# Six triangular solves given whole to one engine each, and a start without 320 zero products

## The chip, the cores and the metric

One core of one Trainium2 chip (trn2) runs the whole program in one launch. The metric is device time in microseconds of one execution; smaller is better. The core has five engines that run their own instruction queues in order: TensorE (PE; matrix products into PSUM; its weight loads are listed apart, as PEld), VectorE (DVE), ScalarE (ACT), GpSimd (POOL) and SyncE (SP), which here issues nearly all the DMAs.

## The reference

Three layers follow each other. The first is a delta-rule attention with B, H, S, D = 4, 8, 768, 48, a recurrence over 768 tokens with a 48 x 48 state per head:

```python
k_n = k / (norm(k) + 1e-06)
for t in range(S):
    y[:, :, t] = einsum('bhd,bhde->bhe', q[:, :, t], state)
    v_old = einsum('bhde,bhd->bhe', state, k_n[:, :, t])
    state = state + beta[t] * einsum('bhd,bhe->bhde', k_n[:, :, t], v[:, :, t] - v_old)
```

Its output, 3072 tokens of 384 numbers, goes through a mixture of 8 experts (each takes exactly 384 tokens, assigned greedily by sorted router logits; ReLU between two matrices) and then through a dense layer, `silu(h @ w_in) @ w_out` with 2048 hidden numbers. All inputs are float32.

## The kernel before, in words

**Attention by chunks.** The 768 tokens are cut into 24 chunks of C = 32. Within a chunk the recurrence becomes a triangular system of 32 equations per head. For each chunk `prep` loads q and k (L371 and, for the first four chunks, L364) and splits them into two fp16 halves (L373 on ScalarE, L374 on VectorE), and DMAs copy the halves to other partitions (L379); `gram` multiplies k with k and q with k on TensorE (L396) and evicts (L403, L405, L409, L410). Each operand of a product is a pair of fp16 halves, so every product is made of three.

**The solves.** Four chunks make a group, six groups in all; `tgroup(g)` inverts the 32 x 32 triangular matrices of a group, all 128 of them at once: a partition holds one matrix. It transposes the gram numbers into L (L421, VectorE), works out the norms (L425 to L436), scales L (L439, VectorE), and prepares X: multiplication (L448), triangular mask (L451, always GpSimd), diagonal (L454, always GpSimd). Then for j = 1 to 30 it multiplies row j of L with column j of X (L462, into a scratch) and adds this to X (L465): n columns by 31 - j rows, where n is at most j. Each step needs the one before it. At the end X is transposed back (L468, VectorE, two instructions) and split into fp16 halves (L475, L477) for the steps.

There is one X for all groups, so L448 of a group waits for L468 of the group before. L exists twice.

`SPLIT` says who solves: before, the first 4, 5, 6 or 10 columns of X go to VectorE and the others to GpSimd. Columns don't depend on each other, and each engine has its own scratch, so the two parts run side by side.

**The steps.** `stage(c)` loads k and v of chunk c (L485), splits k (L488, L489), scales v (L492, on VectorE or GpSimd, whichever the planner finds earlier), and copies eleven pieces into slots for TensorE with four DMAs (L497, about 1 MB). The slots exist twice, so the copies for chunk c + 2 wait until step c has been read. `step(c)` is the recurrence itself, for two halves of the heads: state times k (L527) and times q (L537), the inverted matrix (L548), the new state (L563), the chunk's output (L574); between these are fp16 splits on ScalarE and VectorE (L502 and L503) or on ScalarE and TensorE (L507 to L510). `gate(c)` makes the router's logits. Step c + 1 needs the state of step c.

**Start.** At the beginning `shapes` has TensorE make ten lots of 32 products of a zero tile, in five array shapes (L212); the planner charges 1.0 us for a lot. Their results are not used. `warm` gives 300 more zero products (L192, 128 x 256), each at the lowest priority, which the planner puts where TensorE would have nothing to do.

**Order.** The order of the instructions of every engine is fixed before the run, by a list scheduler (`Plan.order`): each operation is entered with its engine or engines, a cost, what it reads and writes, and a priority; the one that is ready first and has the longest tail behind it goes next. For a VectorE operation of n elements the cost is 0.07 + 0.00104 n, for GpSimd 0.075 + 0.002 n, and from one operation to the next that needs it on the same engine 0.127 and 0.102 us are added. SyncE's DMA issues are planned in the same way and stand in one queue. On the chip each engine takes its own queue in that order; an instruction whose operands are late holds up those behind it.

**Experts and dense layer.** They follow on the same engines. Between attention and the first expert there is a search for the tokens of that expert, on VectorE mostly; the weights are loaded and split (L801 to L810 for the dense layer), part of it in buffers that take the place of attention's L and X.

Of the kernel before, what the change touches and what calls it, by code (L numbers as in the profile page):

```python
# [20 lines left out]
C = 32  # L21
# [10 lines left out]
N6 = 3  # L32
FH = 0.0
KF = 2
SPLIT = (
    (("DVE", 0, 6), ("Pool", 6, C)),
    (("DVE", 0, 5), ("Pool", 5, C)),
    (("DVE", 0, 4), ("Pool", 4, C)),
    (("DVE", 0, 5), ("Pool", 5, C)),
    (("DVE", 0, 4), ("Pool", 4, C)),  # L40
    (("DVE", 0, 10), ("Pool", 10, C)),
)
GROUPS = tuple(tuple(range(c, c + 4)) for c in range(0, NCH, 4))
SX, SWG = 6, 10

# [143 lines left out]
def warm(P, nc, bank, z, n, r, w):  # L189

    for _ in range(n):
        P.op("PE", WC, lambda e: nc.tensor.matmul(bank[:, 0:256], z[:, 0:128], z[:, 128:], start=True, stop=True),  # L192
             r=r, w=w, prio=-1e6, look=(1.0, 0.0))


def shapes(P, nc, banks, z, r, w):

    T = nc.tensor
    forms = (
        (1, lambda i: (slice(0, 128), slice(0, 128), 0)),  # L200
        (2, lambda i: (slice(64 * i, 64 * i + 64), slice(64 * i, 64 * i + 64), 0)),
        (2, lambda i: (slice(64 * i, 64 * i + 64), slice(0, 128), i)),
        (4, lambda i: (slice(32 * i, 32 * i + 32), slice(32 * i, 32 * i + 32), 0)),
        (2, lambda i: (slice(0, 128), slice(64 * i, 64 * i + 64), 0)),
    )

    for n, (k, form) in enumerate(2 * forms):
        def go(e, n=n, k=k, form=form):
            for j in range(32):
                rows, cols, b = form(j % k)  # L210
                at = 48 * (j // k % 8)
                T.matmul(banks[b][cols, at:at + 48], z[rows, 0:cols.stop - cols.start], z[rows, 128:176], start=True, stop=True)  # L212
        P.op("PE", 1.0, go, r=r, w=w, prio=HOT)


class Arena:


# [43 lines left out]
def act(n, sb=True):  # L262
    return 0.055 + 0.00083 * n + (0.043 if sb else 0.0)
# [10 lines left out]
def attention(tc, P, ar, sh, kq, kv, bt, cst, idh, wg, xs):  # L274
    nc = tc.nc
    V, A, G, T = nc.vector, nc.scalar, nc.gpsimd, nc.tensor
    E = {"DVE": V, "Pool": G}
# [29 lines left out]
    wz = ar.new(["wz"], [384], F16)  # L307
# [14 lines left out]
    def sta(t, at, Q):  # L322
        return t[:, at, Q // 4].rearrange("p s (i q) -> p (s i) q", q=4)[:, :, Q % 4]
# [12 lines left out]

    P.op("DVE", 0.2, lambda e: V.memset(wz, 0.0), w=["wz"])
    P.op("Pool", 0.1, lambda e: G.memset(tiny, 1e-30), w=["tiny"])
    shapes(P, nc, ar.banks[4:6], wz, ["wz"], [("y", 0), ("y", 1)])
    warm(P, nc, ar.banks[5], wz, WARM, ["wz"], [("y", 1)])  # L340
    P.op("DVE", 4.3, fill(gsl, "p x c g s n -> p (x c g s n)"), w=["gsl"])
    for t, k in ((rsl[1][:, 0:8], 1), (rsl[1][:, 8:], 1), (rsl[0][:, 0:8], 0), (rsl[0][:, 8:], 0)):
# [40 lines left out]
    def gram(c):  # L383
# [8 lines left out]
        def mm(e, Q):  # L392
            n = 0
            for t in range(2):
                for a, b in P3:
                    T.matmul(gp_[:, Q], sta(gs[:, x], 2 * a + t, Q), cv[:, :, b, t, Q // 4, :, Q % 4], start=(n == 0), stop=(n == 5))  # L396
                    n += 1
# [15 lines left out]
    def tgroup(g):  # L413
# [24 lines left out]
        for k in range(2):  # L438
# [3 lines left out]
             r=["nb0"], w=["nb1"])  # L442
        parts = [(k, en, k0, k1) for k, (en, k0, k1) in enumerate(SPLIT[g])]
        xk = [("X", k) for k in range(2)]
# [61 lines left out]
    def split_pe(hi, lo, acc, ident, s, n, kp, kh, kl):  # L506
        P.op("ACT", act(n, False), lambda e: A.activation(hi, acc, AF.Copy, scale=s), r=[kp], w=[kh])  # L507
        P.op("PE", 0.01 + n / 2400, lambda e: T.matmul(acc, ident, hi, start=False, stop=True, skip_group_check=True),
             r=["idl", kh], w=[kp])
        P.op("ACT", act(n, False), lambda e: A.activation(lo, acc, AF.Copy, scale=s), r=[kp], w=[kl])  # L510

    def step(c):
        x = c % 2
        rs, y = rsl[x], yp[x]
        for g in range(2):
            w_, u_, n_, wu_, st_ = wt[g], ut[g], ns[g], wu[g], st[g]

            def vin(e, g=g, wu_=wu_):
                T.matmul(wu_[:, 0], ids, kr[x][:, 8 + 4 * g:12 + 4 * g, :], start=True, stop=(c == 0))

            P.op("PE", 0.38, vin, r=["ids", ("kv", x, 0)], w=[("wu", g)], prio=LEAD["vin"])
            if c:
                def kn(e, bs, last, g=g, wu_=wu_, n_=n_):
                    for a, b in bs:
                        for Q in range(4):
                            for t in range(2):
                                T.matmul(wu_[:, 0, Q], sta(rs, KR[x] + 2 * a + t, 4 * g + Q), n_[:, b, t, Q, :],  # L527
                                         start=False, stop=(last and (a, b) == P3[-1] and Q == 3 and t == 1))
# [178 lines left out]
HOT = 1000.0  # L707
# [511 lines left out]
def _program(ins):  # L1219
    import concourse.bacc as bacc  # L1220

    nc = bacc.Bacc("TRN2", target_bir_lowering=False, num_devices=1)
    d = {k: nc.dram_tensor(f"in_{k}", a.shape, mybir.dt.from_np(a.dtype), kind="ExternalInput").ap()
         for k, a in ins.items()}
    out = nc.dram_tensor("out_0", _OUT, F32, kind="ExternalOutput").ap()
    with tile.TileContext(nc) as tc, ExitStack() as ctx:
        dram = ctx.enter_context(tc.tile_pool(name="dram", bufs=1, space=DRAM))
        xs = dram.tile([NTOK, 2 * DM], F16, name="xs")
        plan = Plan()
        ar = Arena(ctx, tc, plan, 212832)  # L1230
        ar.at(210852)
        sh = shared_tiles(ar)
        ar.at(0)
        plan.base, plan.look = 9.0 * HOT, LOOK
        attention(tc, plan, ar, sh, d["kq"], d["kv"], d["bt"], d["cst"], d["idl"], d["wg"], xs)
        moe(tc, plan, ar, sh, xs, d["w1"], d["w2"], d["win"], d["wout"], d["mch"], out)
        with tc.manual_schedule():
            plan.emit()
    return nc
# [22 lines left out]
```

## Time and profile before

| what | us |
|---|---|
| median of three runs (lowest, highest) | 1064.65 (1058.99, 1065.28) |
| the profiled execution | 1064.36 |
| its span, first to last instruction | 1062.7 |
| busy in the span: PE, PEld | 935.5, 676.6 |
| busy: DVE, ACT, POOL | 719.7, 491.1, 395.8 |
| PE busy with the 320 zero products | 7.9 |
| DVE busy with L462 and L465, 180 instructions each | 59.9, 62.1 |
| POOL busy with L462 and L465, 146 instructions each | 64.9, 71.5 |

Attention ends about 376 us into the span; the experts and the dense layer take the rest. Busy time is added up over the instructions of an engine. "Idle before" is idle time of the engine directly before an instruction, with what ended it; an instruction with little of it didn't hold its engine up. The granted clock of TensorE is a share of 2.4 GHz.

### The profile page before, as it was taken

To read this page: it belongs to the slowest core of one execution; us is meant where nothing else is said; L and a number is where in the kernel's file an instruction comes from. 1 tells how busy PE (TensorE), PEld (TensorE's weight loads), DVE (VectorE), ACT (ScalarE), POOL (GpSimd) and SP (SyncE) were. 2 spreads that over 40 slices of the span, in tenths; PEclk is the share of its full clock that TensorE was granted. 3 is DMA by queue.
4 is the path that set the end of the run, shared out by engine and by line. 5 is a ranking of instruction groups with operands and counts; after the bars stand their busy time and mean duration, and the time that the engine had idled before them with its cause. 6 is when DMAs were issued, how large, how long until landed. Compare 5 with 4: busy or idle time off the path is not lost.

```text
span 1062.7 us, 27011 instructions
## 1 busy us (share of the span) xinstructions
PE 935.5 (88%) x11073; PEld 676.6 (64%) x11073; DVE 719.7 (68%) x1852; ACT 491.1 (46%) x970; POOL 395.8 (37%) x515
## 2 busy tenths in 40 slices
PE   6987989988897831978998999998998999899997
PEld 6867889888887821544665565665665666566664
DVE  5898888888875587999558458558458457442250
ACT  4314446464555542656436337336336336742250
POOL 6578565747452253375204204203104103202011
PEclk9989899998988965898999999999999999999999
DMA  7428497877787736232203203103103104501000
GB/s 224 112 57 195 109 215 171 197 187 182 185 168 172 182 104 219 84 107 87 78 1 96 69 1 112 53 2 116 49 2 112 53 1 123 160 2 38 9 1 23
DMA packets 178796, 107.72 MB, mean 101 GB/s; under 512 B 141552, under 2 KB 162416, under 8 KB 178672
## 3 DMA queue, kind: packets, MB, share of 16 engines
q1 hardware_dynamic: 175600, 96.55, 35.3%
q0 software_dynamic: 3072, 9.44, 2.6%
q8 instruction: 87, 1.43, 0.5%
q14 instruction: 37, 0.30, 0.1%
HBM read 65.07 MB, written 9.44 MB: 70 GB/s over the span
## 4 chain that ended last, share of the span: by engine, by line
PE 56%; DVE 20%; DMA 9%; POOL 4%; issue 3%; SPq 3%; ACT 2%; POOLq 0%; DVEq 0%; ACTq 0%
PE bank L1138 44%; DMA sb<-sb 4%; PE bank L396 3%; SPq L497 2%; DVE sb L917 2%; DVE sb L465 2%; DVE sb L462 2%; PE bank L527 2%; DMA sb<-in_kv 2%; POOL sb L465 2%; POOL sb L462 1%; PE bank L537 1%; PE bank L563 1%; DMA sb<-in_kq 1%; DMA sb<-xs,sb 1%
## 5 line engine op out<-in xcount | busy, mean ns | idle before, releaser
L1138 PE MATMUL bank<-sb 128*128 128x384 f16 x3456 | 593.6, 330 | 0.0
L1138 PEld LDWEIGHTS <-sb 128*128 128x128 f16 x3456 | 328.4, 99 | 211.5 <-issue 11.8
L1178 POOL TENSOR_TENSOR sb<-sb 128x384 f16<-128x384 f32 x43 | 42.3, 984 | 301.3 <-ACT sb L1177 215.7
L1177 ACT ACTIVATE sb<-sb 128x384 f16<-128x384 f32 x128 | 66.3, 521 | 52.6 <-DVE sb L1175 51.5
L396 PE MATMUL bank<-sb 128*128 128x64 f16 x1152 | 75.4, 242 | 12.2 <-DVE sb L374 5.0
L396 PEld LDWEIGHTS <-sb 128*128 128x128 f16 x1152 | 72.4, 119 | 14.5 <-issue 14.2
L1175 DVE SCALAR_TENSOR_TENSOR sb<-bank,sb 128x384 f32<-128x384 f32 x128 | 69.7, 550 | 15.1 <-ACT sb L1174 14.7
L1174 ACT ACTIVATE sb<-bank 128x384 f32<-128x384 f32 x128 | 61.3, 480 | 33.0 <-PE bank L1138 32.2
L465 POOL TENSOR_TENSOR sb<-sb 128x126 f32<-128x126 f32 (+22 forms) x146 | 71.5, 489 | 11.0
L502 ACT ACTIVATE sb<-bank 128x192 f16<-128x192 f32 (+1 forms) x118 | 45.8, 391 | 59.0 <-PE bank L527 32.6
L503 DVE SCALAR_TENSOR_TENSOR sb<-bank,sb 128x192 f16<-128x192 f32 (+1 forms) x118 | 49.5, 428 | 32.2 <-ACT sb L502 31.9
L1178 DVE TENSOR_TENSOR sb<-sb 128x384 f16<-128x384 f32 x85 | 51.1, 605 | 26.5 <-ACT sb L1177 25.6
L462 POOL TENSOR_TENSOR sb<-sb 128x126 f32<-128x126 f32 (+22 forms) x146 | 64.9, 445 | 10.5
L527 PE MATMUL bank<-sb 128*128 128x48 f16 x1104 | 47.5, 198 | 23.5 <-DMA sb<-sb 22.6
L465 DVE TENSOR_TENSOR sb<-sb 128x30 f32<-128x30 f32 (+23 forms) x180 | 62.1, 345 | 3.3
L1187 POOL DMA_INDIRECT out<-sb x24 | 24.8, 1034 | 100.6 <-ACT sb L1185 81.9
L462 DVE TENSOR_TENSOR sb<-sb 128x30 f32<-128x30 f32 (+23 forms) x180 | 59.9, 333 | 3.0
L527 PEld LDWEIGHTS <-sb 128*128 128x128 f16 x1104 | 44.2, 118 | 27.6 <-issue 25.0
L1064 ACT ACTIVATE sb<-sb 128x768 f32<-128x768 f32 x56 | 46.6, 838 | 27.8 <-DMA sb<-in_w 25.7
L1149 DVE SCALAR_TENSOR_TENSOR sb<-bank,sb 128x384 f16<-128x384 f32 x64 | 35.5, 555 | 31.9 <-ACT sb L1148 31.6
L1148 ACT ACTIVATE sb<-bank 128x384 f16<-128x384 f32 x64 | 31.4, 490 | 51.7 <-PE bank L1138 44.7
L563 PE MATMUL bank<-sb 128*128 128x48 f16 x1104 | 47.4, 193 | 5.2 <-ACT sb L502 3.3
(158 smaller groups left out, 1498.4 us busy)
## 6 DMA issues: line engine op xcount, KB each, us to landing
sb<-sb SPq DMA_DIRECT2D x96, 256.0 KB, 5.5
sb<-in_w SPq DMA_DIRECT2D x64, 384.0 KB, 5.1
sb<-in_kq SPq DMA_DIRECT2D x40, 256.0 KB, 4.2
sb<-in_kv SPq DMA_DIRECT2D x24, 384.0 KB, 4.9
sb<-sb SPq DMA_DIRECT2D x48, 128.0 KB, 3.7
sb<-in_win SPq DMA_DIRECT2D x8, 768.0 KB, 5.6
sb<-in_wout SPq DMA_DIRECT2D x8, 768.0 KB, 5.8
xs<-sb SPq DMA_DIRECT2D x48, 96.0 KB, 3.5
```

Of the source, the lines that this page charges most:

```text
L396: T.matmul(gp_[:, Q], sta(gs[:, x], 2 * a + t, Q), cv[:, :, b, t, Q // 4, :, Q % 4], start=(n == 0), stop=(n == 5))
L462: P.op(en, cost[en](n * m), lambda e, x=x, t=t, j=j, n=n, m=m: E[e].tensor_tensor(t, L[:, j:j + 1, j + 1:].to_broadcast([128, n, m]), x[:, ...
L465: P.op(en, cost[en](n * m), lambda e, x=x, t=t, j=j: E[e].tensor_tensor(x[:, :, j + 1:], x[:, :, j + 1:], t, op=OP.add), r=[("tmp", en)], ...
L503: P.op("DVE", dve(n), lambda e: V.scalar_tensor_tensor(lo, src, s, hi, op0=OP.mult, op1=OP.subtract), r=[r, wh], w=[wl])
L527: T.matmul(wu_[:, 0, Q], sta(rs, KR[x] + 2 * a + t, 4 * g + Q), n_[:, b, t, Q, :], start=False, stop=(last and (a, b) == P3[-1] and Q == 3 ...
L563: T.matmul(st_[:, t, Q], sta(rs, nat(x, a, t), 4 * g + Q), u_[:, b, Q], start=(c == 0 and n == 0 and Q == 0 and t == 0), stop=False, skip_ ...
L1064: op("ACT", act(n), lambda e: A.activation(st3, st3, AF.Copy, scale=2.0 ** s), [], [("stg", i)])
L1138: T.matmul(bk[:, :N], lw(a), rw(b), start=(first and n == 0), stop=(last and n == 2))
L1174: op("ACT", act(N, False), lambda e, bk=bk, y=y: A.activation(sg[y], bk[:, :N], AF.Sigmoid, scale=s3), [kbk], [("sg", y)])
L1175: v(dve(N), lambda e, bk=bk, y=y: V.scalar_tensor_tensor(gf[y], bk[:, :N], s3 * 2.0 ** SG, sg[y], op0=OP.mult, op1=OP.mult), [kbk, ("sg", ...
L1177: op("ACT", act(N), lambda e, f=f, y=y: A.activation(gT[:, 0, f], gf[y], AF.Copy), [("gf", y)], [("gT", f, 0)])
L1178: op({"DVE": dve(N), "Pool": pool(N)}, 0, lambda e, f=f, y=y: EN[e].tensor_tensor(gT[:, 1, f], gf[y], gT[:, 0, f], op=OP.subtract), [("gf" ...
```

## The change

`SPLIT` now names one engine for each group: VectorE for group 0, GpSimd for groups 1 to 5, each for all 32 columns. There is then one first multiplication, one mask and one diagonal a group instead of two, and 60 instructions in the recurrence, of up to 240 elements. The function `shapes` and its call are gone. Since all operations are planned together, the order on every engine is worked out anew.

```diff
-SPLIT = (
-    (("DVE", 0, 6), ("Pool", 6, C)),
-    (("DVE", 0, 5), ("Pool", 5, C)),
-    (("DVE", 0, 4), ("Pool", 4, C)),
-    (("DVE", 0, 5), ("Pool", 5, C)),
-    (("DVE", 0, 4), ("Pool", 4, C)),
-    (("DVE", 0, 10), ("Pool", 10, C)),
-)
+SPLIT = ((("DVE", 0, C),),) + 5 * ((("Pool", 0, C),),)
...
-def shapes(P, nc, banks, z, r, w):
...
-    for n, (k, form) in enumerate(2 * forms):
-        def go(e, n=n, k=k, form=form):
-            for j in range(32):
-                rows, cols, b = form(j % k)
-                at = 48 * (j // k % 8)
-                T.matmul(banks[b][cols, at:at + 48], z[rows, 0:cols.stop - cols.start], z[rows, 128:176], start=True, stop=True)
-        P.op("PE", 1.0, go, r=r, w=w, prio=HOT)
...
-    shapes(P, nc, ar.banks[4:6], wz, ["wz"], [("y", 0), ("y", 1)])
     warm(P, nc, ar.banks[5], wz, WARM, ["wz"], [("y", 1)])
```

## Rows read from the trace of the kernel before

**Rows 1.** Busy time by stretch: stretch, length, busy us and instructions, clock, DMA.
```profile
130.00:335.00 205.00, 182.95 (x4230) 176.67 (x4227) 165.82 (x447) 109.27 (x264) 116.00 (x217) 0.93 0.81 183
335.00:376.00 41.00, 34.46 (x861) 33.37 (x862) 22.23 (x43) 23.25 (x51) 14.18 (x10) 0.88 0.77 181
376.00:424.00 48.00, 8.60 (x138) 5.63 (x137) 40.85 (x102) 17.59 (x23) 22.94 (x12) 0.54 0.51 164
```
**Rows 2.** Timeline of TensorE, state products (L527): start us, length us, engine, line.
```profile
128.19 0.95 PE L527 MATMUL bank<-sb 128*128 128x48 f16 x24
...
335.47 0.72 PE L527 MATMUL bank<-sb 128*128 128x48 f16 x16 [1.14 <-DMA sb<-sb]
...
368.22 0.69 PE L527 MATMUL bank<-sb 128*128 128x48 f16 x16 [1.72 <-DMA sb<-sb]
```
**Rows 3.** Timeline, handovers from one solve to the next, and one preparation.
```profile
73.45 2.00 POOL L448 TENSOR_TENSOR sb<-sb 128x864 f32<-128x864 f32 x1 [4.60 <-DVE sb L468]
...
176.46 1.83 POOL L448 TENSOR_TENSOR sb<-sb 128x864 f32<-128x864 f32 x1 [3.27 <-DVE sb L441]
...
180.95 0.22 POOL L462 TENSOR_TENSOR sb<-sb 128x25 f32<-128x25 f32 x1
...
277.28 2.15 DVE L468 STREAM_TRANSPOSE sb<-sb 128x512 f32<-128x512 f32 x2
279.51 1.60 POOL L448 TENSOR_TENSOR sb<-sb 128x704 f32<-128x704 f32 x1 [2.50 <-DVE sb L468]
...
323.76 2.18 DVE L468 STREAM_TRANSPOSE sb<-sb 128x512 f32<-128x512 f32 x2
```
**Rows 4.** Timeline of solve 0.
```profile
37.93 1.97 POOL L448 TENSOR_TENSOR sb<-sb 128x832 f32<-128x832 f32 x1 [0.72 <-DVE sb L441]
...
43.80 0.25 DVE L462 TENSOR_TENSOR sb<-sb 128x30 f32<-128x30 f32 x1
...
71.42 1.95 DVE L468 STREAM_TRANSPOSE sb<-sb 128x512 f32<-128x512 f32 x2
```
**Rows 5.** Groups by line, VectorE, 43.8 to 71.4: busy us, mean ns, idle before.
```profile
L465 DVE TENSOR_TENSOR sb<-sb 128x30 f32<-128x30 f32 (+26 forms) x30 | 10.9, 363 | 0.8
L462 DVE TENSOR_TENSOR sb<-sb 128x30 f32<-128x30 f32 (+26 forms) x30 | 10.6, 352 | 0.7
```
**Rows 6.** Timeline of VectorE in solve 5, where GpSimd's part is over.
```profile
313.48 0.27 DVE L462 TENSOR_TENSOR sb<-sb 128x100 f32<-128x100 f32 x1
313.78 0.26 DVE L465 TENSOR_TENSOR sb<-sb 128x100 f32<-128x100 f32 x1
...
321.43 0.18 DVE L462 TENSOR_TENSOR sb<-sb 128x10 f32<-128x10 f32 x1
321.64 0.18 DVE L465 TENSOR_TENSOR sb<-sb 128x10 f32<-128x10 f32 x1
```
**Rows 7.** Timeline of the start: the zero products, and ScalarE's wait.
```profile
6.22 7.91 PE L212 MATMUL bank<-sb 128*128 128x48 f16 x320 [6.22 <-DVE sb L337]
...
20.88 1.26 ACT L373 ACTIVATE sb<-sb 128x512 f16<-128x512 f32 x2 [10.50 <-DMA sb<-in_kq]
```
**Rows 8.** Timeline: the last burst of fillers, and the slot copies for step 4.
```profile
107.96 7.69 PE L192 MATMUL bank<-sb 128*128 128x256 f16 x57
...
129.57 5.37 SPq L497 DMA_DIRECT2D sb<-sb  x4
```
**Rows 9.** Timeline of GpSimd, consecutive solve instructions of solves 0 and 3.
```profile
42.91 0.22 POOL L462 TENSOR_TENSOR sb<-sb 128x24 f32<-128x24 f32 x1
43.21 0.23 POOL L465 TENSOR_TENSOR sb<-sb 128x24 f32<-128x24 f32 x1
...
193.77 0.52 POOL L465 TENSOR_TENSOR sb<-sb 128x168 f32<-128x168 f32 x1
194.37 0.50 POOL L462 TENSOR_TENSOR sb<-sb 128x169 f32<-128x169 f32 x1
```
**Rows 10.** Groups by line, GpSimd, 119 to 279: busy us, mean ns, idle before.
```profile
L492 POOL TENSOR_TENSOR sb<-sb 128x384 f32<-128x384 f32 x8 | 7.3, 916 | 27.8 <-DMA sb<-in_kv 27.8
...
L410 POOL TENSOR_TENSOR sb<-sb 128x256 f16<-128x256 f32 x4 | 2.7, 680 | 9.1 <-ACT sb L409 8.1 <-DMA sb<-sb 1.0
```

More of the change, by code (lines that the diff above doesn't have):

```diff
@@ L193, in warm @@
              r=r, w=w, prio=-1e6, look=(1.0, 0.0))
-def shapes(P, nc, banks, z, r, w):
[L198 to L205, printed above, removed]
-    for n, (k, form) in enumerate(2 * forms):
-        def go(e, n=n, k=k, form=form):
-            for j in range(32):
-                rows, cols, b = form(j % k)
-                at = 48 * (j // k % 8)
-                T.matmul(banks[b][cols, at:at + 48], z[rows, 0:cols.stop - cols.start], z[rows, 128:176], start=True, stop=True)
-        P.op("PE", 1.0, go, r=r, w=w, prio=HOT)
 class Arena:
```

## The prediction, made before the changed kernel ran

> **What bounds the kernel now.** I first cut the span into stages with the table of busy time by stretch. The long middle stretch, in which most of the 24 attention steps run, has TensorE busy for 182.95 of 205 us, 89%, at a mean clock share of 0.93 (a mixture of the 1.2 and 2.4 GHz levels), and VectorE for 165.82 of 205; GpSimd has 116.00 [rows 1]. So TensorE alone could shorten this stretch by at most 11%, and nothing after it gets shorter by this change; what attention gains, the end of the program gains.
>
> Then I asked what sets the pace of the steps. Step 4 begins its first state products at 128.19, step 20 at 335.47, step 23 at 368.22 [rows 2]: 12.95 us a step while solves run, (368.22 - 335.47)/3 = 10.9 us a step when they are over. Something that belongs to the solves costs about 2 us a step. The reader should see the handovers next: a solve's first multiplication (L448) starts right behind the transposes (L468) of the solve before it, because X exists once. From the first handover at 73.45 to the end of the last transposes at 323.76 + 2.18 = 325.94 five solves pass, 50.5 us each [rows 3]. Four steps last 4 x 12.95 = 51.8 us. Solves and steps run at one pace, and either may be pulling the other.
>
> **The change, part by part.**
>
> *Solve 0 on VectorE.* Now it lasts from 37.93 (L448) to 71.42 (L468), 33.5 us [rows 4]. VectorE's share of it is 10.9 + 10.6 = 21.5 us in 60 instructions [rows 5]; 71.42 - 43.80 - 21.5 = 6.1 us between them is other VectorE work. A VectorE instruction of a solve follows its predecessor after 0.30 us at 100 elements and 0.21 us at 10 [rows 6], so 0.20 + 0.0010 n. The whole recurrence is 30 steps of j(31 - j) elements, 4960 in all, twice (multiply, add): 60 instructions and 9920 elements, 12.0 + 9.9 = 21.9 us. VectorE alone therefore needs what its share costs now beside a working GpSimd. With the first multiplication (0.20 + 1024 x 0.0010 = 1.2 us), the mask and the diagonal still on GpSimd (at most 180.95 - 176.46 - 1.83 = 2.7 us [rows 3]) and the other work of 6.1 us I get 31.9 us: 1.6 us less. Bounds: nothing, if other work is put in between more often, and 6 us less, if GpSimd takes that work. I take -2.
>
> *The zero products.* They hold TensorE for 7.91 us from 6.22 on, and its queue goes on with products that need copied operands [rows 7]. ScalarE then sits idle for 10.50 us, until 20.88, before a conversion whose load was late; evictions of the first gram products stand behind it in its queue. With the zero products gone the planner, which charged 10 us for them, can place these evictions earlier. Between 0 and 7.9 us; I take -2, near the lower end, since the operands' copies and the loads are not touched.
>
> *The fillers.* The 300 filler products are dealt out by the planner to TensorE's planned idle time. With the zero products gone some are used at the beginning, where TensorE would otherwise sit idle (7.91/0.135 is about 58, at the 7.69 us of 57 fillers late in the stage), and are missing from the last burst, which starts at 107.96 and stands in front of step 2; the slot copies for step 4 are issued at 129.57 [rows 8]. Between 0 and -7.7 us for steps 2 to 4. I cost it at nothing in the sum, because step 4 also waits for solve 1, below; without that cover it is a gain of up to 5 us for steps 2 to 4. The opposite is not excluded: fewer fillers later leave TensorE idle, and where it is idle most of the time, as between 376 and 424, the granted clock is 0.54, near the 1.2 GHz level [rows 1]; I take the length of the burst, 7.7 us, as the most of that.
>
> *Solves 1 to 5 on GpSimd.* Its solve instructions follow each other after 0.30 us at 24 elements and 0.60 us at 168 [rows 9]: 0.25 + 0.0021 n, so 60 x 0.25 + 9920 x 0.0021 = 36 us. The preparation takes 180.95 - 176.46 = 4.5 us for two pieces and some 4.3 for one; the transposes and the hop to the next L448 take 279.51 - 277.28 = 2.2 us [rows 3]. Other GpSimd work costs 7.3 + 2.7 = 10.0 us in 160 us [rows 10], 3 us a period. Sum: 36 + 4.3 + 2.2 + 3 = 45.5 us, against 50.5.
>
> *A wait that is added.* VectorE's transposes L468 now wait for another engine. Behind them in VectorE's queue stand the fp16 splits of the running step, and TensorE's next products wait for those. The planner's prices make this solve 60 x (0.075 + 0.102) + 9920 x 0.002 = 30.5 us, 5.5 us less than my 36, so it places the transposes too early. Between 0 (steps are late as well) and 5.5 us a handover; I take 3, the middle. Period 48.5 us, 2 us below now, five times: -10.
>
> *VectorE relieved.* 20 us of solve work a period leave VectorE. I cost it at nothing: of the two engines in the step's chain TensorE is fuller. SyncE's order of loads and slot copies is planned anew too; no row prices that, and I give it 4 us either way.
>
> **Sum**: -2 - 2 - 10 = -14 us. The profiled execution took 1064.36 us (span 1062.7 and 1.66 around it), 0.29 us below the median of 1064.65, so 1050.
>
> **Rivals.**
> *Slower: solves stuck behind a load.* L492, the scaling of v, waits on GpSimd for its DMA: 27.8 us of idle time in 160 us [rows 10], 8.8 us a period. Now GpSimd's part of a solve has room for that; alone, it would stand in the solve's own chain. At full price the period is 45.5 + 8.8 = 54.3 us, 5 x 3.8 = +19 us, less 4 at the start: 1079; at half price, with my 3 us for the transposes, 52.9 us: +12 - 4, 1072. It decides from a period of 51.3 us, where the start's 4 us are used up. For it: eight of these waits exist. Against: the planner may give L492 to VectorE, which gets empty. 0.20.
> The Trainium skill, GPSIMD Engine Reference, section 4.1 (Engine selection), speaks against this change: two-input elementwise work belongs on VectorE, GpSimd being about 2 times slower. By that a solve on GpSimd would be 2 x 21.9 = 44 us, an estimate, and the period 56 us, which is this rival's result by another road (1064 - 4 + 5 x 6 = 1090); the rows make the ratio 36/21.9 = 1.6, so I leave that result 0.03 of the 0.20.
>
> *No difference.* The steps set the pace and solves only follow: TensorE's 89%, and slot copies that are issued four at a time by one queue. Then only the start's -4 stays: 1060. 0.27. That the zero products' place is simply filled by fillers belongs here.
>
> *Much faster.* The full 45.5 us a period: -25, and -4 at the start: 1035; TensorE's bound is 205 - 182.95 = 22 us, so 1064 - 22 - 4 = 1038. Then solve 5 ends some 25 us earlier, and weight conversions, whose buffers it frees, start sooner. 0.13.
>
> **How the numbers follow.** Forecast 0.40, with its own range 1042 to 1054. A time counts as a difference when it is more than 1% from 1064.65, below 1054.0 or above 1075.3, about what measurement can tell here. Faster: 0.40 + 0.13 = 0.53. Of the slower rival's 0.20 some 0.05 lie at half price, below that bound, but other orders of the queues can lose as much, which I count in its place: 0.20. Same 0.27. The range leaves out the far half of "much faster" and of "slower": 1035 to 1075.
>
> **What would show it.** Right: GpSimd's L448 to L448 at 46 to 50 us; L468 of solve 5 ending near 312 instead of 325.94; steps 4 to 20 at 12.3 us. Wrong: VectorE idle before L468 for 5 us or more on GpSimd, with splits late behind it; GpSimd idle before L492 between two solve instructions; periods above 51 us; or short periods with an unchanged 12.9 us a step.

## The result: slower, and the profile after

The changed kernel took 1077.48 us (median of 4 runs, 1075.48 to 1078.61), the kernel before 1063.36 (4 runs): ratio 1.0137, 95% interval 1.010 to 1.0173. The forecast was 1050, the range 1035 to 1075. The profiled execution took 1077.1 us, span 1075.4. The 28 lines that went out move the numbers: L440 is the old L468 (transposes), L420 the old L448, L434 and L437 the old L462 and L465, L449 the old L477, L464 the old L492, L469 the old L497 (slot copies), L475 the old L503, L499 the old L527 (state products).

Busy time by stretch in the kernel after (columns as in [rows 1]); attention now ends near 395 us:

```profile
130.00:335.00 205.00, 172.53 (x3844) 165.90 (x3842) 112.77 (x221) 95.73 (x230) 144.58 (x247) 0.88 0.77 169
...
395.00:440.00 45.00, 9.68 (x139) 6.92 (x140) 38.10 (x102) 15.39 (x21) 19.54 (x11) 0.51 0.52 165
```

Against [rows 1], VectorE lost 53 us of work in the 205 us, GpSimd took on 29, and TensorE did less, at a clock share of 0.88 instead of 0.93: it waits more. The timeline of TensorE (state products of steps 3, 4, 20 and 23) says where:

```profile
118.05 0.42 PE L499 MATMUL bank<-sb 128*128 128x48 f16 x8 [2.74 <-DMA sb<-sb]
...
138.70 0.48 PE L499 MATMUL bank<-sb 128*128 128x48 f16 x9 [1.79 <-DMA sb<-sb]
...
357.82 0.76 PE L499 MATMUL bank<-sb 128*128 128x48 f16 x15 [7.77 <-DMA sb<-sb]
...
386.85 0.32 PE L499 MATMUL bank<-sb 128*128 128x48 f16 x5 [1.70 <-DMA sb<-sb]
```

The same steps of the kernel before began at 128.19, 139.14 (the row just below), 335.47 and 368.22 [rows 2]. Up to step 3 the change is 10 us ahead; step 4 has lost that; steps 4 to 20 take 13.7 us each instead of 12.3; step 23 is 18.6 us late. From its state products to the end the kernel after needs 5.9 us less (span less start: 688.6 against 694.5), so the span grows by 12.7.

```profile
139.14 0.55 PE L527 MATMUL bank<-sb 128*128 128x48 f16 x12 [1.82 <-DMA sb<-sb]
```

What holds the groups up is in the timeline of GpSimd, VectorE and SyncE's DMA queue around the end of solve 3 in the kernel after, with the steps' splits (L475) between:

```profile
226.34 0.27 POOL L437 TENSOR_TENSOR sb<-sb 128x30 f32<-128x30 f32 x1
...
237.19 0.36 DVE L475 SCALAR_TENSOR_TENSOR sb<-bank,sb 128x192 f16<-128x192 f32 x1 [0.66 <-ACT sb L474]
...
240.75 0.56 DVE L475 SCALAR_TENSOR_TENSOR sb<-bank,sb 128x384 f16<-128x384 f32 x1
241.22 2.07 DVE L440 STREAM_TRANSPOSE sb<-sb 128x512 f32<-128x512 f32 x2
...
243.37 1.93 POOL L420 TENSOR_TENSOR sb<-sb 128x1024 f32<-128x1024 f32 x1 [16.75 <-DVE sb L440]
...
245.60 10.06 SPq L469 DMA_DIRECT2D sb<-sb  x8
```

The solve is done at 226.61. Its transposes start at 241.22, because in VectorE's queue they stand behind the splits of step 11, the last of the group before. GpSimd is idle for 16.75 us; the slot copies of step 12, and behind them those of step 13, go out only at 245.60, after the splits of the transposed X (L449). Step 12 begins at 254.22. In the kernel before the solve's last instruction and its transposes at this place lay close together, with one step split (L503) between:

```profile
224.36 0.15 DVE L465 TENSOR_TENSOR sb<-sb 128x5 f32<-128x5 f32 x1
...
224.52 0.55 DVE L503 SCALAR_TENSOR_TENSOR sb<-bank,sb 128x384 f16<-128x384 f32 x1
224.98 2.13 DVE L468 STREAM_TRANSPOSE sb<-sb 128x512 f32<-128x512 f32 x2
```

The waits of 60 to 350 us show all handovers from one solve to the next (us in total, times, longest), first of the kernel before, then of the kernel after:

```profile
POOL sb L448 <- DVE sb L468: 15.6, 4, 4.6
```
```profile
POOL sb L420 <- DVE sb L440: 51.3, 5, 16.8
...
SPq L469 <- DVE sb L449: 16.1, 5, 5.1
```

Each wait of GpSimd holds the 2 us of the transposes themselves, and the first of the five, 5.35 us, is for solve 0, which ran on VectorE. From the end of a solve to the start of its transposes solves 1 to 5 lose 5.1, 12.2, 14.6, 8.5 and 9.1 us; in the kernel before it was at most 2.3, and the fifth wait, 3.3 us, ended with L441.

In the order of VectorE's instructions the transposes of solves 1 to 5 stood behind 8 (the second of them 9), 34, 54, 73 and 95 step splits in the kernel before, and stand behind 18, 39, 59, 79 and 100 after. A step has five splits: they moved by two steps in solve 1 and by about one in the others, to the very end of the step ahead of the group that needs them.

### The profile page after: what moved, and what is told of

Read it like the earlier page. It is cut to its first block, busy times and chain, and to the rows that moved or that the text cites. A ratio compares the mean times of both kernels' runs of the same rounds, so it can differ in the third digit from the quotient of the medians.

```text
span 1075.4 us, 26009 instructions
## 1 busy us (share of the span) xinstructions
PE 930.7 (87%) x10753; PEld 672.6 (63%) x10753; DVE 653.6 (61%) x1581; ACT 485.7 (45%) x959; POOL 400.5 (37%) x487
## 4 chain that ended last, share of the span: by engine, by line
PE 60%; DVE 16%; DMA 11%; SPq 5%; issue 3%; ACT 3%; POOL 1%; POOLq 0%; DVEq 0%; ACTq 0%
PE bank L1110 43%; DMA sb<-sb 8%; SPq L469 4%; PE bank L368 4%; PE bank L499 3%; DVE sb L889 2%; PE bank L509 2%; PE bank L535 2%; PE bank L185 2%; DMA sb<-in_kq 1%; DMA sb<-xs,sb 1%; DVE sb L449 1%; PE bank L546 1%; PE bank L491 1%; DVE sb L779 1%
## 5 line engine op out<-in xcount | busy, mean ns | idle before, releaser
L1110 PEld LDWEIGHTS <-sb 128*128 128x128 f16 x3456 | 328.5, 99 | 212.0 <-issue 12.6
L475 DVE SCALAR_TENSOR_TENSOR sb<-bank,sb 128x192 f16<-128x192 f32 (+1 forms) x118 | 49.9, 428 | 72.7 <-ACT sb L474 72.3
L437 POOL TENSOR_TENSOR sb<-sb 128x30 f32<-128x30 f32 (+9 forms) x150 | 85.6, 571 | 11.8
L434 POOL TENSOR_TENSOR sb<-sb 128x30 f32<-128x30 f32 (+9 forms) x150 | 82.7, 551 | 11.3
L368 PEld LDWEIGHTS <-sb 128*128 128x128 f16 x1152 | 72.8, 118 | 6.4 <-issue 6.1
L1146 ACT ACTIVATE sb<-bank 128x384 f32<-128x384 f32 x128 | 61.4, 480 | 32.2 <-PE bank L1110 31.4
L499 PE MATMUL bank<-sb 128*128 128x48 f16 x1104 | 46.0, 198 | 30.0 <-DMA sb<-sb 28.6
L499 PEld LDWEIGHTS <-sb 128*128 128x128 f16 x1104 | 43.4, 118 | 32.8 <-issue 25.8
L346 DVE SCALAR_TENSOR_TENSOR sb<-sb 128x512 f16<-128x512 f32 x48 | 36.6, 782 | 34.3 <-ACT sb L345 29.4
L1121 DVE SCALAR_TENSOR_TENSOR sb<-bank,sb 128x384 f16<-128x384 f32 x64 | 35.5, 555 | 32.4 <-ACT sb L1120 32.2
L889 DVE TENSOR_TENSOR sb<-sb 128x192 f16<-128x192 f16 (+3 forms) x116 | 51.3, 476 | 1.1
L535 PEld LDWEIGHTS <-sb 128*128 128x128 f16 x1104 | 45.5, 118 | 10.0 <-issue 9.4
```

The costliest lines, as they stand in the source:

```text
L434: P.op(en, cost[en](n * m), lambda e, x=x, t=t, j=j, n=n, m=m: E[e].tensor_tensor(t, L[:, j:j + 1, j + 1:].to_broadcast([128, n, m]), x[:, ...
L437: P.op(en, cost[en](n * m), lambda e, x=x, t=t, j=j: E[e].tensor_tensor(x[:, :, j + 1:], x[:, :, j + 1:], t, op=OP.add), r=[("tmp", en)], ...
L475: P.op("DVE", dve(n), lambda e: V.scalar_tensor_tensor(lo, src, s, hi, op0=OP.mult, op1=OP.subtract), r=[r, wh], w=[wl])
L535: T.matmul(st_[:, t, Q], sta(rs, nat(x, a, t), 4 * g + Q), u_[:, b, Q], start=(c == 0 and n == 0 and Q == 0 and t == 0), stop=False, skip_ ...
L889: V.tensor_tensor(mv, a, iota2[:, None, 0:J].to_broadcast([128, h, J, 2]), op=o)
L1110: T.matmul(bk[:, :N], lw(a), rw(b), start=(first and n == 0), stop=(last and n == 2))
```

## The experiments

Theory A: the loss is the late place of the transposes. Rivals: B, a solve on GpSimd is itself too slow; C, leaving out the zero products costs; D, the steps have a pace of their own, which no faster solve betters. All times are medians, ratios against the kernel before, which ran beside them (1063.62 for the first four, 1062.83 for the next four, 1064.5 for the ninth).

**1. Zero products out, solves split as before.**
```diff
-    shapes(P, nc, ar.banks[4:6], wz, ["wz"], [("y", 0), ("y", 1)])
```


> The kernel before with the 320 zero products left out and the solves split by columns as before. Theory A (the loss of the change comes from where the transposes of a finished solve stand in VectorE's queue, and the zero products are innocent): no loss; steps 2 and 3 begin 8 to 12 us earlier, as in the changed kernel, and since the split solves hand over at the planned place at least part of it stays: 1050 to 1060 us, ratio 0.987 to 0.997. Theory C (leaving out the zero products costs, by fillers used up early and a lower clock): 1067 to 1077 us. In both, the state products of step 3 near 118 instead of 128.

1054.68 us, ratio 0.990 (0.9863 to 0.9936). C is out: alone, this half of the change gains 9 us. Steps 2 and 3 begin at 104.75 and 115.97 (before: 117.49 and 128.19), 12.7 and 12.2 us earlier. The timeline of TensorE shows what moved: more fillers went to the beginning, the products of the first four chunks run in one piece, and no burst stands before step 2 (none of it is left after 95.77):

```profile
6.24 8.18 PE L192 MATMUL bank<-sb 128*128 128x256 f16 x52 [6.24 <-DVE sb L337]
14.26 12.14 PE L395 MATMUL bank<-sb 128*128 128x64 f16 x192
...
95.77 0.27 PE L192 MATMUL bank<-sb 128*128 128x256 f16 x1
```

That these moves are due to the missing products, and not only to a plan made anew, is not shown: experiment 2 keeps the products and has an early start too, and experiment 8 lacks them and gains 1 us.

**2. Solves whole, zero products kept.**
```diff
-SPLIT = (
-    (("DVE", 0, 6), ("Pool", 6, C)),
...
-)
+SPLIT = ((("DVE", 0, C),),) + 5 * ((("Pool", 0, C),),)
```


> The kernel before with only the solves given whole to one engine; the 320 zero products stay. Theory A: the transposes stand again at the end of the step before the group that needs them, GpSimd is idle 5 to 15 us before each next solve, time 1075 to 1088 us (the changed kernel's 1077, or up to 10 more as the early gain of steps 2 and 3 is missing). Theory C: near 1063, since the zero products are there.

1078.55 us, ratio 1.0162 (1.0114 to 1.021); GpSimd waits 60.3 us for the transposes in five waits. The early gain, which was expected to be missing, is there: steps 2 and 3 begin at 110.60 and 120.27, 7 and 8 us earlier than in the kernel before, and here too no burst of fillers stands before step 2. Step 4 begins at 141.40, 10.6 us after the end of solve 1's transposes (130.76); in the changed kernel it begins at 138.70, 10.4 us after them (128.26). So the two halves don't add: with the zero products or without, the time is that of the whole change, since step 4 waits for solve 1 in both.

**3. The same plan, the solve's end moved up in VectorE's queue.** The order that the planner found is kept; only the operations of a solve, its transposes and splits are sorted in at 0.75 of their planned distance from the solve's start. TensorE's and SyncE's queues are the same, instruction for instruction.
```diff
+    solves, HOIST = (), 0.75
...
+        for a, b in self.solves:
+            for i in range(a, b):
+                at[i] = self.start[a] + self.HOIST * (self.start[i] - self.start[a])
+        seq = sorted(seq, key=lambda i: (at[i], i))
```


> The changed kernel with one thing moved: within the order that the planner found, the solve of groups 1 to 5, its transposes and the splits behind them stand earlier, by a quarter of the time that the planner gives from the solve's first instruction; the queues of TensorE and SyncE stay exactly as they are. Theory A (transposes too late in VectorE's queue): GpSimd's idle time before the next solve falls from 51 us in five waits to under 15, the period of the solves from 55 to 42 to 48 us, and the time by 12 to 25 us, to 1052 to 1066. Theory B (a solve on GpSimd is itself too slow, 40 us of chain): the period stays above 50 us, VectorE now waits before the transposes with step work queued behind, and the time is 1075 or more.

1070.96 us, ratio 1.006 (1.004 to 1.008), against 1.0137: 6.5 us of the 14 come back by this alone. The transposes stand behind 12, 33, 53, 73 and 95 splits (the second one of solves 1 and 5 behind one more), nearly as in the kernel before. But the time, the wait and the period miss what A expected: GpSimd still waits 32.2 us before its solves (26.8 of it put down to L423, the end of the next group's scaling, which also stands in VectorE's queue and was not moved), the period is (333.73 - 70.92)/5 = 52.6 us, and the last three transposes still start 7 to 10 us after the end of their solve. VectorE at that place, solve 3 (over at 214.68; here L488 is the split, L451 the transposes):

```profile
217.15 0.69 DVE L356 SCALAR_TENSOR_TENSOR sb<-sb 128x512 f16<-128x512 f32 x1 [3.33 <-ACT sb L355]
...
223.47 0.36 DVE L488 SCALAR_TENSOR_TENSOR sb<-bank,sb 128x192 f16<-128x192 f32 x1 [0.65 <-ACT sb L487]
223.75 1.13 DVE L451 STREAM_TRANSPOSE sb<-sb 128x512 f32<-128x512 f32 x1
```

What stands ahead of them is itself late. I put that down to the other queues, which were planned around a late handover and which this run leaves as they are; no run shows it. B is not borne out, though the period stayed above its 50 us: VectorE has no wait for GpSimd before these transposes.

**4. Everything planned anew, with the solve priced lower.**
```diff
-        cost = {"DVE": dve, "Pool": pool}
+        cost = {"DVE": dve, "Pool": lambda n: 0.8 * pool(n)}
```


> The changed kernel with the planner's price of the solve's operations times 0.8, nothing else; the whole order is planned anew, and the transposes stand four to ten step splits earlier in VectorE's queue (about one step). Theory A: as with the moved transposes, 1050 to 1066 us. Theory B: 1075 or more, with VectorE idle before the transposes.

1060.9 us, ratio 0.9964 (0.9941 to 0.9987). The waits of GpSimd from 60 to 350 us:

```profile
POOL sb L420 <- DVE sb L440: 10.5, 1, 10.5
```

The same solves on the same engine, 17 us faster; the transposes start at most 3.6 us after the end of their solve. A solve on GpSimd is not too slow, B is out. But this is no faster than experiment 1 with its split solves.

**5. Most of the recurrence left out.**
```diff
-        for j in range(1, C - 1):
+        for j in range(1, C - 1 if g == 0 else 3):
```


> The changed kernel with most of the recurrence left out for groups 1 to 5 (steps j = 3 to 30, 56 of 60 instructions a solve), so that its attention is not the reference's; preparation, transposes and splits stay. A solve then costs GpSimd about 5 us. It shows the pace of the steps without solves. Theory D (the steps have a pace of their own of about 12.2 us, set by slot copies, TensorE and the queues, so that faster solves could never have given the forecast gain): steps 4 to 20 at 11.8 to 12.4 us each, attention about as long as in the kernel before, time 1045 to 1058. Rival (the solves set the pace, as the prediction's sum had it): steps at 11 us or less, time 1025 to 1040.

1040.73 us, ratio 0.9803 (0.9763 to 0.9843). The time lies between the two ranges, 4 us below D's and 0.7 above the rival's; the pace is what D expected. State products of steps 4 and 20:

```profile
124.26 0.52 PE L499 MATMUL bank<-sb 128*128 128x48 f16 x11 [2.26 <-issue]
...
321.42 0.45 PE L499 MATMUL bank<-sb 128*128 128x48 f16 x9
```

(321.42 - 124.26)/16 = 12.3 us, the pace of the kernel before, with hardly a solve left. The gain is before step 4 (14.9 us earlier than 139.14) and after the steps, not in their pace. D's pace holds; what sets it is not shown by this run.

**6. The slot copies priced higher, the solve's price untouched.**
```diff
-        dma(1.05e6, slots, ...
+        dma(1.8e6, slots, ...
```


> The changed kernel with the planner's price of the slot copies' transfer 1.7 times as high (1.8 for 1.05 MB), nothing else; the solve's price is as it was. Planned steps get slower instead of planned solves faster; the transposes stand 1 to 6 splits earlier in VectorE's queue for groups 1 to 5 (14, 36, 53, 73, 99 against 18, 39, 59, 79, 100). Theory A (only the planned place of the solve's end against the steps matters, by whichever price it comes): 1055 to 1068 us, GpSimd's wait for the transposes under 30 us, the last group still late. Rival (the GpSimd price itself matters): within 4 us of the changed kernel's 1077.

1058.56 us, ratio 0.9967 (0.995 to 0.9984); GpSimd waits 10.9 us for the transposes. In the changed kernel, what counts is where the planner believes the solve's end to lie against the steps, by whichever price. Experiments 4 and 6 plan every queue anew, so they show the place of the transposes together with the rest of a plan; only experiment 3 moves the solve's end alone.

**7. Solve 0 on VectorE, the others split, no zero products.**
```diff
-    (("DVE", 0, 6), ("Pool", 6, C)),
+    (("DVE", 0, C),),
```


> The kernel before without the zero products, solve 0 on VectorE alone, the other five split by columns as before: the change without its GpSimd part. Theory A: like the kernel without zero products, 1050 to 1058 us, solve 0's transposes ending 0 to 2 us earlier than with the split. Rival (solve 0 on one engine costs, since its 60 instructions are longer): 1060 or more.

1055.02 us, ratio 0.9919 (0.9899 to 0.994), the same as experiment 1. The transposes of solve 0 end at 72.95 us, at 71.72 in experiment 1: VectorE alone gains nothing, where 0 to 2 us were expected.

**8. The lower price with split solves.** Experiment 1 with 0.8 on both engines' prices.
```diff
-        cost = {"DVE": dve, "Pool": pool}
+        cost = {"DVE": lambda n: 0.8 * dve(n), "Pool": lambda n: 0.8 * pool(n)}
```

> The kernel before without the zero products and with the planner's price of the solve's operations times 0.8 on both engines. With split solves the transposes don't come late (they stand at 13, 33, 53, 71, 94 step splits, 16, 36, 54, 73, 95 without the lower price), so theory A expects little: 1048 to 1060 us. If the price as such were what helped in the changed kernel, this would gain another 10 us, to 1045 or less.

1061.8 us, ratio 0.9983 (0.996 to 1.0005): no gain, rather 7 us lost against experiment 1, and 1.8 us above the range expected, although the transposes stand 1 to 3 splits earlier. A lower price is no good in itself. What costs the 7 us no run shows; a new plan can by itself move the time by that much, so the 9 us of experiment 1 belong to its plan as much as to the missing products.

**9. Half of the slot copies**, on top of experiment 5.
```diff
-            for h in range(4):
+            for h in range(2):
```


> The kernel without most of the recurrence, and of the four slot copies of each chunk only two (the other partitions keep older values, so its attention is not the reference's); the planned order is the same on TensorE, VectorE, ScalarE and GpSimd. If the slot copies (about 4.4 us to issue four and 5.5 us to land, once per two buffers) set the steps' pace of 12.3 us, halving them takes 2 us or more of issue out of the cycle of two steps: pace of steps 4 to 20 at 11.3 us or less, time 15 to 25 us below the 1040.7 without recurrence. If TensorE's work or the split chain sets it, the pace stays above 12 us and the time within 6 us.

997.14 us, ratio 0.9363 (0.9313 to 0.9414). That is 43.6 us below experiment 5, more than the 15 to 25 expected. Steps 4 to 20 take (282.39 - 115.84)/16 = 10.4 us. The busy time between 130 and 290 us, columns as in [rows 1]:

```profile
130.00:290.00 160.00, 159.98 (x3920) 157.44 (x3917) 95.26 (x202) 106.47 (x250) 38.45 (x48) 1.00 0.71 174
```

TensorE is never idle and keeps the 2.4 GHz level. With four copies the slot copies set the pace of 12.3 us, with two TensorE does, at 10.4. This holds for the kernel without most of the recurrence; that the slot copies set the same pace in the kernel before is inferred.

## Why the prediction was wrong, point by point

**The step that failed** is "A wait that is added", with the sum's -10 built on it. It said that the planner places the transposes too early, that VectorE would wait for GpSimd, and took 3 us a handover. It compared the planner's 30.5 us for a solve with my 36, and had no row for the other side: how much slower than planned the steps run; "steps are late as well" was its best case, at 0. The wait came, turned round: GpSimd waited for VectorE, 51.3 us in five handovers against 15.6 in four before, and the slot copies behind it. The period became (348.30 - 70.93)/5 = 55.5 us instead of the forecast 48.5 (transposes 5 end at 348.30, L420 of solve 1 starts at 70.93). The prediction's 0.20 for slower counted "other orders of the queues" in, but gave them no price.

**"Steps follow the solves"** was the second fault, and would have spoiled the forecast even with the handovers in time. Experiments 4 and 6 have periods of 50.0 and 50.2 us, transposes at most 3.6 and 5.1 us late, and steps at 12.2 and 12.4 us; experiment 5 has next to no solves and 12.3. A late solve holds the steps up; an early one lets them start earlier, but doesn't quicken them. The rival "no difference" had this mechanism, and I gave it 0.27. Part of it was a miscount: the row at 128.19 [rows 2] is step 3, not step 4 (each step from step 1 on has 48 state products; steps 1 and 2 begin at 90.56 and 117.49). Steps 4 to 20 took 196.3/16 = 12.3 us, not 12.95, so four steps, 49 us, already fitted inside a period of 50.5, and the 12.3 us named as a sign of being right was the pace of the kernel before. Nor are the 10.9 us of the last three steps the pace without solves: experiment 5 has 11.0 there, behind 12.3. And the bound of 11% that TensorE's busy time seemed to set took its clock share of 0.93 as given: at 1.00 experiment 9 takes 10.4 us a step, 15% less than 12.3.

**Solves on GpSimd**, 36 us and 4.3 of preparation: right. Solves 2 to 5 took 37.0 to 39.0 us from first to last instruction, preparation 3.6. Solve 1 took 46.2: a gram instruction (L382), which waited 6.89 us for ScalarE, stood between two of its own for 7.5 us. The slower rival's load in the solve's way was not what cost the time: L464 waited on GpSimd 10.6 us in two waits, the planner having put 19 of these 24 instructions on VectorE, 7 before. Nor did the result by the Trainium skill's rule (GPSIMD Engine Reference, section 4.1: GpSimd about 2 times slower for two-input elementwise work) come about: the solve's 60 instructions keep GpSimd busy for 34 us and VectorE for 20.3, a ratio of 1.7, and the loss was not GpSimd's rate.

**Solve 0**, -2: the transposes end at 70.79 instead of 73.37, -2.6 us, but by luck. The solve starts at 33.51 instead of 37.93 and lasts longer, 35.3 us instead of 33.5 (31.9 was forecast). With the zero products gone alone it is -1.6 (experiment 1), with VectorE alone +0.4 (experiment 2, 73.80): nothing comes from VectorE.

**Zero products and fillers**, -2 and nothing: mis-sized alone, where the kernel without the products gains 9 us (experiment 1); in the change the cover that I named, solve 1, took all of it: 10 us ahead at step 3, none at step 4 (118.05 and 138.70). That sentence was right for the kernel after. In the kernel before solve 1's transposes were over at 119.19, 10 us before the slot copies of step 4 went out [rows 8], so there it didn't hold step 4.

What stays open: why of the 18.6 us at step 23 only 12.7 are left at the end, beyond that weight conversions overlap the tail of attention; which queue besides VectorE's holds the rest of experiment 3's loss; and what costs experiment 8 its 7 us.

## What to carry to other kernels

Where a written-out order feeds in-order engines, moving work to another engine also moves every instruction that hands it on; look where the hand-over will stand in the receiver's queue, and compare the planner's error on both sides, not on the moved work alone. Before pricing a gain in one of two coupled chains, ask whether the other has a pace of its own: leaving the work out altogether, in one run, tells it. Two parts of one change should be timed alone, since one can hide the other: here one gained 9 us and the other lost 15, and together they lost 14.

## What was not expected of the hardware

Halving the slot copies lets TensorE run without a gap for 160 us at a granted clock of 1.00, where the same stretch (130 to 290 us) had gaps and a share of 0.85 to 0.95 in the ten other profiles. VectorE's 60 solve instructions of all columns take 20.3 us of busy time with GpSimd nearly idle (L434 and L437 in solve 0 of the kernel after), and the 60 shorter ones of 6 columns took 21.5 beside GpSimd [rows 5]: 9920 elements against 4720, twice as many, for about the same time.
